# Squares between exps, squares in place, two tiles transposed by DMA, and masks by halves in a fused attention and MLP kernel

## The chip, the cores and the metric

One core of a Trainium2 chip. The metric is the device time of a whole execution in microseconds (us), lower is better. The kernel before takes 318.52 us (median of four runs, 317.75 to 319.37). Each ratio below is the mean time of one kernel's fast runs over that of the other's of the same rounds, on the same chip, so it is not quite the ratio of the medians that are quoted. "Same" means within 2%.

## The reference, cut to what matters

```python
# q, k, v: [8 batches, 8 heads, 576, 64]; s: [8, 8, 576]; w_in: [512, 2048]; w_out: [2048, 512]
scores = q @ k.T / 8                      # per batch and head
cum = cumsum(max(s, 0)); bias = -(cum[i] - cum[j])
scores = where(causal, -1e9, scores + min(bias, 0))
attn = softmax(scores)                    # + 1e-9 in the denominator
x = (attn @ v) as [4608 tokens, 512]
out = gelu(x @ w_in) @ w_out              # exact gelu
```

## The kernel before

The MLP runs in nine chunks of 512 tokens. Its first layer (`l1_item`) needs `xT`, the attention's output transposed; its second layer (`l2_item`) is cut into 16 pieces, and between these pieces stand the attention items of a later batch: in chunk c's second layer that is batch b = c+1. `sc` computes scores and two exps, `mk` masks them, `av` multiplies with v and normalises, `to_xT` transposes one tile of 128 tokens, on TensorE or, for most tiles, by DMA. A batch has 576 tokens and a chunk 512, so the first layer of chunk 1 needs tiles 0 to 3 of batch 1, and that of chunk 2 tiles 0 to 2 of batch 2.

ScalarE also squares q and k of batch 0 and all of v, only for their sums, which a check of the inputs' size uses at the end. The squares' output itself is thrown away:

```python
def square_v(b, st):
    n_st = 128 if st < ST - 1 else SL
    sq = work.tile([128, S * 2], bf16, tag="sq", bufs=1, name="sq")
    nc.scalar.activation(sq[:n_st, : H * D], raws[b, "v"]..., func=AF.Square,
                         accum_out=sumv[:n_st, b, st : st + 1])
# second layer of chunk 0 (b = 1), cut
side[6] = [(scale_v, b, 2), (av, b, 1, 0, True), (mk, b, 0, 1)]
side[7] = [(sc, b, 1, 1), (av, b, 1, 1, True), (to_xT, b, 0, True)]      # True: on TensorE
side[8] = [(scale_v, b, 3), (av, b, 0, 2), (to_xT, b, 1, True), (gelu_set,), (mk, b, 1, 1)]
# second layers of chunks 1 to 6 (b = 2 to 7), cut
sc_at = (2, 5, 7, 9) if b < 4 else (2, 5, 8, 11)
...
for st in range(ST):
    side[sc_at[3]].append((square_v, b, st))
side[sc_at[3]].append((gelu_set,))
```

The loads of v have two buffers. The load for the batch after next waits until the last reader of its buffer is done, and in these chunks that reader is the fifth square. All loads are issued in order on the GpSimd queue; stores and DMA transposes on the sync queue.

## Time and profile before

| | before |
|---|---|
| time, median of 4 runs | 318.52 us |
| span of the profiled run | 316.6 us |
| TensorE busy | 303.5 us |
| clock of TensorE granted in the profile | 1.00 (0.994 to 0.999 in later runs) |

TensorE is busy 96% of the span, so a change must be read by what TensorE waits for.

### The profile page before, as it was taken

Reading aid. Unit: us, or ns where it says so; the run is one execution under the profiler, and the core shown is the slowest. Engines: PE = TensorE matmul, PEld = TensorE weight load, DVE = VectorE, ACT = ScalarE, POOL = GpSimd, SP = SyncE. Lnnn points to the kernel's source line nnn. Section 1 sums busy time; section 2 is a strip of 40 time slices with the busy share of each in tenths; the row PEclk is TensorE's granted clock in tenths of the full one; section 3 lists DMA queues with packets and bytes.
Section 4 is the critical chain, followed back from the end, with each engine's and each line's share of the span. In section 5 each row is a group of like instructions: output and inputs, shape, how many; then the busy total and the mean of one; then the engine's idle time right before and its main releaser. Section 6 shows DMA issues by size and latency. Waiting matters only on the chain. (4 is left out here: it accounts for less than half of the span.)

```text
span 316.6 us, 6078 instructions
## 1 busy us (share of the span) xinstructions
PE 303.5 (96%) x2480; PEld 156.1 (49%) x2523; DVE 199.9 (63%) x400; ACT 192.9 (61%) x256; POOL 52.9 (17%) x72
## 2 busy tenths in 40 slices
PE   8999998999999999999999999999999999999993
PEld 3587754444554455445444444444444545444441
DVE  7876658699769766965697559945894632250020
ACT  2786976887765687564956676657756685105500
POOL 8543440125070006000240004000000000000000
PEclk9999999999999999999999999999999999999999
DMA  7999999669869215932399158412110321010012
GB/s 133 220 230 209 226 212 277 129 111 211 187 176 185 64 53 155 196 59 76 97 176 162 66 101 160 35 56 79 52 24 34 101 51 25 33 69 33 1 69 75
DMA packets 30980, 36.48 MB, mean 115 GB/s; under 512 B 15648, under 2 KB 20000, under 8 KB 30944
## 3 DMA queue, kind: packets, MB, share of 16 engines
q0 software_dynamic: 11552, 23.07, 38.5%
q1 hardware_dynamic: 19248, 12.80, 15.7%
q8 instruction: 22, 0.36, 0.5%
q14 instruction: 14, 0.11, 0.2%
q10 hardware_dynamic: 144, 0.13, 0.1%
HBM read 36.85 MB, written 9.44 MB: 146 GB/s over the span
## 5 line engine op out<-in xcount | busy, mean ns | idle before, releaser
L466 PE MATMUL h_ps<-xT,w_in_r 128*128 128x512 bf16 (+1 forms) x626 | 131.7, 357 | 2.8 <-ACT gT L471 2.0
L482 PE MATMUL o_ps<-w_out_r,gT 128*128 128x512 bf16 x549 | 132.3, 379 | 2.2 <-issue 1.3
L471 ACT ACTIVATE gT<-h_ps 128x1024 bf16<-128x1024 f32 (+1 forms) x80 | 74.6, 938 | 63.7 <-PE h_ps L466 62.9
L466 PEld LDWEIGHTS <-w_in_r 128*128 128x128 bf16 x640 | 60.0, 98 | 56.5 <-issue 2.9
L482 PEld LDWEIGHTS <-gT 128*128 128x128 bf16 x576 | 52.0, 98 | 56.5 <-issue 3.1
L358 ACT ACTIVATE P<-sc_ps 128x1024 bf16<-128x1024 f32 x56 | 54.3, 1021 | 30.7 <-PE sc_ps L343 30.7
L122 POOL DMA_DIRECT2D raw_v<-in_v_dram x40 | 34.0, 864 | 119.7 <-ACT sq L212 107.4
L492 DVE COPY o_sb<-o_ps 128x512 f32<-128x512 f32 x32 | 22.1, 691 | 48.5 <-PE o_ps L482 48.5
L443 DVE RECIPROCAL rc<-av 128x4 f32<-128x4 f32 (+1 forms) x80 | 14.0, 175 | 40.2 <-PE av L434 40.2
L187 DVE STREAM_TRANSPOSE qkT<-raw_qk 128x576 f32<-128x576 f32 x32 | 37.4, 1242 | 0.9 <-DMA raw_qk<-in_k_dram 0.6
L434 PEld LDWEIGHTS <-P 128*128 128x128 bf16 x576 | 27.2, 98 | 17.4 <-DVE x L444 1.6
L444 DVE TENSOR_TENSOR x<-av,rc 128x256 bf16<-128x256 f32 (+1 forms) x80 | 33.8, 423 | 3.0
L204 DVE TENSOR_REDUCE amx<-raw_qk 128x2 f32<-128x2304 bf16 x14 | 35.1, 2535 | 0.0
L434 PE MATMUL av<-vv,P 128*128 128x65 bf16 x576 | 30.4, 193 | 1.0 <-DVE x L444 0.7
L220 DVE TENSOR_TENSOR vv<-raw_v,wb 128x512 bf16<-128x512 f32 (+1 forms) x40 | 26.0, 689 | 3.2 <-DMA raw_v<-in_v_dram 3.2
L366 DVE TENSOR_TENSOR P<-P,tri_bf 128x1024 bf16<-128x1024 bf16 x32 | 21.9, 684 | 8.8 <-ACT P L358 8.8
L212 ACT ACTIVATE sq<-raw_v 128x512 bf16<-128x512 f32 (+1 forms) x40 | 25.1, 628 | 0.8
L343 PE MATMUL sc_ps<-qkT 32*128 32x256 bf16 (+2 forms) x560 | 18.2, 250 | 0.1
L343 PEld LDWEIGHTS <-qkT 32*128 32x128 bf16 x560 | 11.7, 92 | 12.7 <-issue 12.0
L418 PE MATMUL f_ps<-zero 128*128 128x512 bf16 x32 | 11.2, 468 | 1.3 <-DVE zero L150 1.2
L497 ACT ACT_TABLE_LOAD x8 | 10.3, 1283 | 0.9 <-PEq L819 0.7
L500 ACT ACT_TABLE_LOAD x8 | 10.3, 1283 | 0.1
(79 smaller groups left out, 90.2 us busy)
## 6 DMA issues: line engine op xcount, KB each, us to landing
out_dram<-o_sb SPq DMA_DIRECT2D x35, 256.0 KB, 2.2
raw_v<-in_v_dram POOLq DMA_DIRECT2D x32, 256.0 KB, 6.3
raw_qk<-in_q_dram POOLq DMA_DIRECT2D x7, 576.0 KB, 9.0
raw_qk<-in_k_dram POOLq DMA_DIRECT2D x7, 576.0 KB, 11.9
w_in_r<-in_moe_w_in_dram POOLq DMA_DIRECT2D x4, 512.0 KB, 12.0
w_out_r<-in_moe_w_out_dram POOLq DMA_DIRECT2D x4, 512.0 KB, 16.4
raw_v<-in_v_dram POOLq DMA_DIRECT2D x8, 128.0 KB, 8.0
raw_qk<-in_q_dram POOLq DMA_DIRECT2D x2, 288.0 KB, 5.6
```

The costliest lines, as they stand in the source:

```text
L122: eng.dma_start(out=t[:n_st, st, :, :], in_=bass.AP(tensor=v.tensor, offset=v.offset + b * H * S * D + st * 128 * D, ap=[[D, n_st], [S * D ...
L187: nc.vector.transpose(qkT[b % 2][:, i, g, :S, :].rearrange("p s e -> p (s e)").bitcast(fp32) .rearrange("p (l j) -> p j l", j=LT), raws[b, ...
L204: nc.vector.tensor_reduce(amx[:, b * HG + g], raws[b, "qk"][:, :, g, :], axis=AX, op=ALU.max, apply_absolute_value=True,)
L212: nc.scalar.activation(sq[:n_st, : H * D], raws[b, "v"][:n_st, st].rearrange("p h d -> p (h d)"), func=AF.Square, accum_out=sumv[:n_st, b, ...
L220: nc.vector.tensor_tensor(vv[b % 2][:n_st, st, :, 0:D], raws[b, "v"][:n_st, st, :, :], w.unsqueeze(2).to_broadcast([n_st, H, D]), op=MULT,)
L343: nc.tensor.matmul(s_ps[h // 2][:, h % 2, off : off + n], lhsT=qk[r, 1, g, jt * 128 : jt * 128 + 128, e], rhs=qk[r, 0, g, i0 : i0 + n, e], ...
L358: nc.scalar.activation(P[:, 2 * h2 : 2 * h2 + 2, o : o + 512], s_ps[h2], func=AF.Exp, scale=scale)
L434: nc.tensor.matmul(o_ps[:, h, :], lhsT=P[:, h, off : off + 128], rhs=vv[b % 2][:, jt, 4 * g + h, :], start=(i == 0), stop=(i == len(BLK[it ...
L444: nc.vector.tensor_tensor(x_of[b, it][:n, g * 256 : g * 256 + 256].rearrange("p (h d) -> p h d", d=D), o_ps[:n, :, 0:D], rc[:n].unsqueeze( ...
L466: nc.tensor.matmul(h_ps[:, i, :], lhsT=w_in_r[:, ko, ft * 128 : (ft + 1) * 128], rhs=xT[:, ko, c * NB + n0 : c * NB + n1], start=(ko == 0) ...
L471: nc.scalar.activation(gT_of[c][:, f2 * 2 : f2 * 2 + 2, n0:n1], h_ps, func=AF.Gelu)
L482: nc.tensor.matmul(y_of[c, sub], lhsT=gT[:, ft, sub * 128 : (sub + 1) * 128], rhs=w_out_r[:, ft, :], start=(ft == 0), stop=(ft == FT - 1),)
```

## The change

Its intent: to fill ScalarE's gaps between exps with the squares of v, so that the gelu after them starts earlier; to take eight transposes of batch 1 off TensorE; to shorten the start of batch 0. The squares of q and k in place free the room for two square buffers.

```diff
     def square_qk(g, i):
-        sq = work.tile([128, S * 2], bf16, tag="sq", bufs=1, name="sq")
+        r = raws[0, "qk"][:, i, g, :]
-            sq, raws[0, "qk"][:, i, g, :], func=AF.Square, scale=D ** -0.5,
+            r, r, func=AF.Square, scale=D ** -0.5,
     def square_v(b, st):
-        sq = work.tile([128, S * 2], bf16, tag="sq", bufs=1, name="sq")
+        sq = work.tile([128, H * D], bf16, tag="sq", bufs=2, name="sq")
     # start of batch 0 (cut): mask by halves, last scores behind the transposes, three fillers fewer
+    mk_item(0, 1, 0, 0, 2)
     av_item(0, 0, 1)
+    mk_item(0, 1, 0, 2, 4)
     sc_first(0, 1, (1,))
-    mk_item(0, 1, 0)
-    sc_first(1, 1, (0,))
+    filler(1)
     ...
     # second layer of chunk 0
-                side[6] = [(scale_v, b, 2), (av, b, 1, 0, True), (mk, b, 0, 1)]
-                side[7] = [(sc, b, 1, 1), (av, b, 1, 1, True), (to_xT, b, 0, True)]
-                side[8] = [(scale_v, b, 3), (av, b, 0, 2), (to_xT, b, 1, True), (gelu_set,), (mk, b, 1, 1)]
+                side[6] = [(av, b, 1, 0), (av, b, 1, 1), (scale_v, b, 2), (mk, b, 0, 1)]
+                side[7] = [(sc, b, 1, 1)]
+                side[8] = [(scale_v, b, 3), (av, b, 0, 2), (gelu_set,), (mk, b, 1, 1)]
     # second layers of chunks 1 to 6
-                for st in range(ST):
-                    side[sc_at[3]].append((square_v, b, st))
+                for st, at in zip(range(ST), (0, 1, 1, 2, 2)):
+                    side[sc_at[at]].append((square_v, b, st))
```

More of the change, by code (lines that the diff above doesn't have):

```diff
@@ L210, in square_v @@
         n_st = 128 if st < ST - 1 else SL
-        sq = work.tile([128, S * 2], bf16, tag="sq", bufs=1, name="sq")
+        sq = work.tile([128, H * D], bf16, tag="sq", bufs=2, name="sq")
         nc.scalar.activation(
-            sq[:n_st, : H * D], raws[b, "v"][:n_st, st].rearrange("p h d -> p (h d)"), func=AF.Square,
+            sq[:n_st], raws[b, "v"][:n_st, st].rearrange("p h d -> p (h d)"), func=AF.Square,
             accum_out=sumv[:n_st, b, st : st + 1],
@@ L360, in sc_item, with mk_item @@
             )
-    def mk_item(b, g, u):
+    def mk_item(b, g, u, h0=0, h1=4):
         P = P_of[b, g]
         o = UO[u]
-        d = P[:, :, o : o + 512].rearrange("p e (g c) -> p e g c", c=256)[:, :, :, 0:128]
+        d = P[:, h0:h1, o : o + 512].rearrange("p e (g c) -> p e g c", c=256)[:, :, :, 0:128]
         nc.vector.tensor_tensor(
-            d, d, tri_bf.unsqueeze(1).unsqueeze(1).to_broadcast([128, 4, 2, 128]), op=MULT
+            d, d, tri_bf.unsqueeze(1).unsqueeze(1).to_broadcast([128, h1 - h0, 2, 128]), op=MULT
         )
@@ L546 @@
     filler(1)
+    mk_item(0, 1, 0, 0, 2)
     av_item(0, 0, 1)
+    mk_item(0, 1, 0, 2, 4)
     sc_first(0, 1, (1,))
-    mk_item(0, 1, 0)
-    sc_first(1, 1, (0,))
+    filler(1)
     av_item(0, 1, 0)
     av_item(0, 1, 1)
+    sc_first(1, 1, (0,), 0)
+    to_xT(0, 0, True)
+    filler(1)
+    to_xT(0, 1, True)
     sc_first(1, 1, (1,), 0)
-    to_xT(0, 0, True)
-    filler(2)
-    to_xT(0, 1, True)
-    filler(2)
     mk_item(0, 0, 1)
```

## The prediction

> **What bounds the kernel now.** I read the busy shares first, then the list of waits, then the table of busy time by stretches, then the timeline of the stretches that the change touches, because an average cannot say what one small move is worth.
>
> ```profile
> PE 303.5 (96%) x2480; PEld 156.1 (49%) x2523; DVE 199.9 (63%) x400; ACT 192.9 (61%) x256; POOL 52.9 (17%) x72
> ...
> ACT gT L471 <- PE h_ps L466: 62.9, 61, 15.2
> ...
> PE h_ps L466 <- ACT gT L471: 2.0, 4, 0.5
> ...
> PE av L434 <- DVE x L444: 0.7, 1, 0.7
> ```
>
> TensorE is busy for 303.5 of 316.6 us, and the other engines spend most of their idle time waiting for it. So the change can win only by taking work off TensorE or by taking away one of its few waits. All its idle time is 13.1 us, of which some 6 us lie at the very start and in the tail, which the change doesn't touch (1.25 us in the first 10 us, 5.4 us in the last 27). The waits that the list names inside the kernel are four of 0.5 us for ScalarE's gelu and one of 0.7 us for VectorE. Even all of them together are far from 2% (6.4 us). The chain that ended last has six pieces within the last 0.7 us and says nothing of the middle. In the table by stretches, 36 to 56 us (second layer of chunk 0) has 19.05 us of TensorE in 20.0 and a DMA share of 1.10: there TensorE and the DMA engines are full at once.
>
> **What the Trainium skill says, and the trace.**
> 1. "TensorE: Matmul & The Clock Gate", table at its head: ScalarE and VectorE run their queue strictly in order. So a square put between two exps delays the later exp if it doesn't fit the gap. The trace agrees: the gelu's table load starts only 0.01 us after the last of five squares that stand before it.
> 2. "ScalarE: Activation LUTs", What ACT_TABLE_LOAD costs: about 1283 ns, and a drain of about 1380 ns. The load agrees (1283 ns). The drain does not show: the load at 156.25 ends at 157.53 and the gelu starts at 157.55. I use 1.28 us.
> 3. "VectorE: DVE Perf Modes", Side-by-side: some 150 cycles fixed per instruction, two results a cycle in the 2x mode. The masks fit: 684 ns for 1024 elements and 283 ns for 256, which is 0.52 ns per element and 0.15 us fixed. A mask of 512 should take 0.42 us, so two halves 0.84 us in place of 0.68.
> 4. "DMA: Bandwidth & Descriptors", Issuing engines are not separate DMA queues: all issuers' transfers share 16 engines and interleave. A DMA transpose (sync queue) lands 2.4 us after its issue where DMA is quiet (issues at 83.9, 116.7 us), but takes 7.7 us at 62.1, 11.1 at 94.7 and 10.8 at 127.6, amid loads at a share near or above 1. The one of 94.7 landed at 105.8; the loads' full stretch had ended at about 104.2. So under load it lands about when the backlog drains.
>
> **The change, part by part.**
>
> **(a) Squares of v, batches 4 to 7** (second layers of chunks 3 to 6). The timeline before:
>
> ```profile
> 150.67 1.94 ACT L358 ACTIVATE P<-sc_ps 128x1024 bf16<-128x1024 f32 x2 [1.70 <-PE sc_ps L343]
> ...
> 152.50 0.63 ACT L212 ACTIVATE sq<-raw_v 128x512 bf16<-128x512 f32 x1
> ...
> 155.51 0.63 ACT L212 ACTIVATE sq<-raw_v 64x512 bf16<-64x512 f32 x1
> ...
> 156.25 1.28 ACT L500 ACT_TABLE_LOAD   x1
> ...
> 157.55 1.94 ACT L471 ACTIVATE gT<-h_ps 128x1024 bf16<-128x1024 f32 x2
> ...
> 158.62 1.89 PE L466 MATMUL h_ps<-xT,w_in_r 128*128 128x512 bf16 x7 [0.50 <-ACT gT L471]
> ```
>
> Five squares at a pitch of 0.76 us (0.63 plus 0.19 for the accumulator's read, less overlap) push the first gelu to 157.55; by then two groups of first-layer results fill both score buffers, and TensorE waits 0.50 us. The timeline has the same at 158.6, 191.8, 224.9 and 258.1: 4 x 0.5 = 2.0 us. After the change the exps come at (2, 5, 8, 11), with gaps of 1.32, 1.70 and 1.70 us between them; one, two and two squares (0.76, 1.52, 1.52 us) fit. The table load moves to 152.5, the gelu is ready at 153.8, before its data. **-2.0 us.**
>
> **(b) Squares of v, batches 2 and 3** (second layers of chunks 1 and 2). Here the exps stand at (2, 5, 7, 9) and the gaps are shorter:
>
> ```profile
> 80.31 1.94 ACT L358 ACTIVATE P<-sc_ps 128x1024 bf16<-128x1024 f32 x2 [0.87 <-PE sc_ps L343]
> ...
> 82.28 0.66 PE L343 MATMUL sc_ps<-qkT 32*128 32x256 bf16 x24
> ...
> 82.96 1.94 ACT L358 ACTIVATE P<-sc_ps 128x1024 bf16<-128x1024 f32 x2 [0.71 <-PE sc_ps L343]
> ```
>
> Two squares (1.52 us) don't fit the gap of 0.87: the exps that started at 80.31 start at about 80.9 and end at 82.85. The next scores, at 82.28, need both score buffers that these exps free. So TensorE waits about 0.6 us where it waited for nothing. In chunk 2 the gap is 0.71 us: 0.8 us late, and scores at 115.16 against exps that ended at 115.12, so 0.7 to 0.75 us. The last exps become some 1.4 us late, but their masks are needed only at 86.9, just in time. The gelu had 1.2 us of idle time before it here, so nothing is won at the end. **+1.3 us.** Also, the last square frees the buffer for the loads of v some 4 us earlier (84.4 in place of 88.5). They then run beside the transposes of 83.9 and 85.2, which the next first layer needs at 89.7; by the store at 90.1, which took 3.4 us amid the same loads, I count on 0 to 0.5 us.
>
> **(c) First tiles of batch 1 by DMA** (second layer of chunk 0). It takes eight 128x128 transposes off TensorE: two groups of four at 0.24 us, 0.5 us. It takes two copies of 0.42 us off VectorE, and with them and the earlier second item the wait of 0.69 us at 48.75, where TensorE waited for an output buffer. Together 1.2 us off TensorE's path before chunk 1, whose first layer had begun at 56.4. But that layer reads columns 512 to 1023, which hold both tiles. The outputs should be ready at about 45.3 and 46.2, so the transposes issue at 45.3 and 46.5, in the middle of the loads: the share is 1.05 at 53, 0.96 at 54, 0.73 at 55 us. By the pattern in point 4 above they land at about 55.5 to 57.5, while TensorE would be ready at about 55. So a new wait of 0.5 to 2.5 us takes the place of what was removed. I take 1.3: **+0.1 us.**
>
> **(d) Start of batch 0.** From the first output item to the first layer at 18.93 there are seven filler matmuls before and four after, at 0.21 us: 0.65 us less. But the start of the layer hangs on VectorE: mask, reciprocal and scaling, transposes, copy (18.45 to 18.87). Halving the mask lets two heads begin early but costs 0.15 us, and the second half now follows the output of tile 1, so it ends at about 16.2 against 16.09. The last scores move behind the transposes, which takes 0.35 us out from in front of them; the first gelu comes about 0.8 us later, which four free buffers of 0.87 us each absorb. **-0.3 us**, uncertain by as much.
>
> **(e) Squares of q and k in place.** Same four instructions of 1.16 us at the same places, one buffer less; no wait in the list is for that buffer. The loads that wait for these squares (10.4 us on the queue) wait as before. **0.**
>
> Sum: -2.0 + 1.3 + 0.3 (loads beside transposes) + 0.1 - 0.3 = -0.6 us. 318.6 becomes **318.0 us**.
>
> **Rivals.**
> - *The DMA transposes come in time.* For it: the stores at 46.5 and 48.2, issued on the same queue under the same load, landed after 7.5 and 7.8 us, so 53 to 54.5 for the transposes. Against it: transposes move in small packets and were the slowest (11 us). Then (c) is worth -1.2 and the time is 316.8.
> - *The transposes are late twice*: at chunk 1 by 2.5 us, and at chunks 2 and 3 because the earlier loads catch them, 1 to 2 us each. For it: 11 us seen at 94.7. Against it: loads of v build their backlog only after some 2 us. Then the time is 320 to 322.
> - *The delayed exps cost nothing.* If the ends of exps and the start of scores have more slack than the modelled matmul times show, (b) is 0 and the time is about 316.7.
>
> **Range and chances.** Combined, the rivals give some 316 to 321; the runs before spread over 1.6 us. Eight in ten: **316.2 to 319.8**. Nothing reaches 6.4 us either way: faster 0.02, same 0.96, slower 0.02.
>
> **What would show it.** (a) is right if the list of waits has no more waits of the first layer for gelu at the start of chunks 4 to 7. (b) is right if the scores have new waits of 0.6 to 0.75 us for exps, twice. (c) is right if the first layer of chunk 1 waits for a DMA transpose of xT, with a landing of 9 to 11 us; it is wrong if it starts at 55 without a wait. (d) shows in the first layer's start against 18.93. The whole is wrong if TensorE's busy time moves by more than the 1.2 us of transposes and fillers, or if a wait of over 2 us appears elsewhere.

## More of the kernel before

From the 40-slice view of the page of before: a digit is the busy share of a slice of 7.9 us in tenths, and PEclk the granted clock in tenths.

```profile
PE   8999998999999999999999999999999999999993
...
PEclk9999999999999999999999999999999999999999
```

There is no slice in which TensorE is less than 80% busy before the tail, nor one with a lowered clock.

## The result, and the profile after

336.2 us (median of four runs, 334.22 to 337.84) against 318.52: ratio 1.0552, 95% interval 1.0488 to 1.0615. The change is 5.5% slower, and the prediction of 318.0 (316.2 to 319.8) was wrong.

The same views of the page after:

```profile
PE 308.1 (93%) x2470; PEld 156.8 (47%) x2512; DVE 199.4 (60%) x399; ACT 189.5 (57%) x256; POOL 52.9 (16%) x72
...
PE   8999996799979998699989998999999999999993
...
PEclk9999999799989999599999999999999999999999
```

TensorE's share fell to 93%, and in three places, at about 60, 98 and 136 us, the granted clock is lowered. TensorE's busy time rose by 4.6 us though it has fewer instructions: some matmuls ran longer. From the list of waits after (us in total, times, longest):

```profile
PE h_ps L467 <- issue: 8.1, 7, 4.0
PE h_ps L467 <- DMA xT<-x: 4.5, 1, 4.5
```

The four waits of 0.5 us for gelu are gone, as predicted. In their place the first layer waits for xT. The profile names the DMA only once; the other waits it puts down to "issue", which means that it found no releaser. The timeline fills that in. After, at the start of chunk 2:

```profile
88.57 4.21 POOL L122 DMA_DIRECT2D raw_v<-in_v_dram  x5 [8.80 <-ACT sq L213]
88.68 2.54 SPq L406 DMA_TRANSPOSE xT<-x  x2
...
96.23 3.03 PE L467 MATMUL h_ps<-xT,w_in_r 128*128 128x512 bf16 x8 [2.13 <-issue]
```

Before, at the same place in the program:

```profile
83.87 2.54 SPq L405 DMA_TRANSPOSE xT<-x  x2
...
88.82 4.20 POOL L122 DMA_DIRECT2D raw_v<-in_v_dram  x5 [13.62 <-ACT sq L212]
...
89.13 1.89 PE L466 MATMUL h_ps<-xT,w_in_r 128*128 128x512 bf16 x8
```

Before, the loads of v came 4.95 us after the first transpose, when both had landed (2.4 and 2.5 us after issue). After, they come 0.1 us before it. Its two transposes land 4.9 and 6.1 us after issue, the second at 96.1 us, and TensorE goes on at 96.23. In chunk 3 it is the same: the second transpose, issued at 127.3, lands 7.9 us later at 135.2, and TensorE goes on at 135.33 after 3.96 us. At the starts of chunks 4 and 5 waits of 0.70 and 0.69 us are left.

At chunk 1, whose tiles are now DMA transposes, the stretches of 2 us after (busy time of each engine with its instruction count, then granted clock, DMA share, GB/s):

```profile
56.00:58.00 2.00, 0.00 (x0) 0.00 (x0) 0.00 (x0) 0.01 (x1) 1.42 (x2) 1.00 1.28 130
58.00:60.00 2.00, 0.28 (x1) 0.14 (x2) 0.00 (x0) 0.00 (x0) 0.00 (x0) 0.82 1.14 242
60.00:62.00 2.00, 1.78 (x5) 0.76 (x5) 0.00 (x0) 0.60 (x1) 0.00 (x0) 0.50 1.10 293
62.00:64.00 2.00, 2.00 (x16) 0.90 (x14) 0.63 (x3) 0.91 (x1) 0.00 (x0) 0.83 1.12 212
```

TensorE stands still for 4.54 us until 59.72, and then the clock stays at half for about 3 us: five matmuls start in 60 to 62 us where eight take 1.89 us at full clock. (Three microseconds at half the clock do the work of 1.5 us; this first layer is 1.46 us longer than before.) VectorE does nothing from 56 to 60 us and ScalarE next to nothing; GpSimd works for 1.42 us.

**Where the 15.8 us of span went.** I cut both timelines at the first matmul of each layer of each chunk and subtracted.

| what | us |
|---|---|
| waits for xT at the starts of chunks 1 to 5: 4.54, 2.13, 3.96, 0.70, 0.69 | +12.0 |
| first layers of chunks 1, 2, 3 longer: 1.46, 1.66, 2.86 | +6.0 |
| second layers of chunks 1 to 4 longer beside these waits: 0.39, 0.61, 0.16, 0.17 | +1.3 |
| tail | +0.5 |
| first layers of chunks 4 to 7 shorter: 4 x 0.65 | -2.6 |
| second layer of chunk 0 without its wait | -1.0 |
| start and first layer of chunk 0 | -0.4 |
| sum | +15.8 |

### The profile page after: what moved, and what is told of

It reads as the page before. It is cut to its first block, busy times and chain, and to the rows that moved or that the text cites. A ratio compares the mean times of both kernels' runs of the same rounds, so it can differ in the third digit from the quotient of the medians.

```text
span 332.4 us, 6053 instructions
## 1 busy us (share of the span) xinstructions
PE 308.1 (93%) x2470; PEld 156.8 (47%) x2512; DVE 199.4 (60%) x399; ACT 189.5 (57%) x256; POOL 52.9 (16%) x72
## 5 line engine op out<-in xcount | busy, mean ns | idle before, releaser
L467 PE MATMUL h_ps<-xT,w_in_r 128*128 128x512 bf16 (+1 forms) x624 | 136.4, 367 | 13.6 <-issue 8.1
L493 DVE COPY o_sb<-o_ps 128x512 f32<-128x512 f32 x32 | 22.1, 691 | 47.6 <-PE o_ps L483 47.6
L435 PEld LDWEIGHTS <-P 128*128 128x128 bf16 x576 | 27.9, 99 | 17.8 <-issue 1.7
L367 DVE TENSOR_TENSOR P<-P,tri_bf 128x1024 bf16<-128x1024 bf16 (+1 forms) x33 | 22.1, 669 | 9.4 <-ACT P L359 9.4
L419 PE MATMUL f_ps<-zero 128*128 128x512 bf16 x29 | 9.5, 452 | 1.2 <-DVE zero L150 1.2
```

The lines of the kernel that those rows point to most:

```text
L435: nc.tensor.matmul(o_ps[:, h, :], lhsT=P[:, h, off : off + 128], rhs=vv[b % 2][:, jt, 4 * g + h, :], start=(i == 0), stop=(i == len(BLK[it ...
L467: nc.tensor.matmul(h_ps[:, i, :], lhsT=w_in_r[:, ko, ft * 128 : (ft + 1) * 128], rhs=xT[:, ko, c * NB + n0 : c * NB + n1], start=(ko == 0) ...
```

## The experiments

Theory after the result: DMA transposes that are in flight together with loads land late, the change makes that happen at three places where TensorE needs them at once, and each long wait also costs half the clock for some microseconds. Rivals: that the delayed exps are what costs; that one wait at chunk 1 shifts everything after it; that the longer first layers come from something other than the clock. All runs gave correct results.

### 1. The two tiles alone (t_tiles)

```diff
 # before, with the three lines of side[6], side[7] and side[8] of the change
```

> The kernel before with part (c) alone: the first two tiles of batch 1 go by DMA transpose. Theory: these transposes are issued at about 45.5 us into a full DMA queue and land some 13 us later, so the first layer of chunk 1 starts at about 60 us in place of 56.6 (a wait of about 4.5 us less 1.0 us of TensorE work removed), and the array's clock is then halved for about 3 us, which makes that first layer 1.5 us longer. Chunks 2 and 3 start without a wait for a transpose. Total about +4.8 us, 323 us. Rival (the three waits of the changed kernel are all a consequence of the first, because it shifts the loads against the transposes): then the waits at chunks 2 and 3 show here too and the time is near 334 us.

Measured: 325.71 us (323.51 to 326.14), ratio 1.0193 (1.0155 to 1.023). The wait is 6.1 us, the second layer of chunk 0 is 5.06 us longer, the first layer of chunk 1 2.31 us longer, and every later layer is within 0.15 us of before. So this part costs some 2% by itself, 6.2 us where I expected 4.8, and the waits at chunks 2 and 3 are not its consequence: that rival falls. Landing of its two transposes (us, least, median, most), from the view of that line:

```profile
DMA to landing us min/median/max: 14.3/14.8/15.4
```

### 2. The squares alone (t_squares)

```diff
-                for st in range(ST):
-                    side[sc_at[3]].append((square_v, b, st))
+                for st, at in zip(range(ST), (0, 1, 1, 2, 2)):
+                    side[sc_at[at]].append((square_v, b, st))
```

> The kernel before with the squares of v of batches 2 to 7 between the exps, and nothing else. Theory: the last square frees the buffer of v earlier, so the loads of v for the batch after next are issued at the same moment as the two DMA transposes of batches 2 and 3; the transposes land 5 to 8 us after issue in place of 2.5 us, the first layers of chunks 2 and 3 wait some 2 and 4 us, and the clock is halved after each wait (some 1.6 and 2.9 us). Against it stand 4 x 0.65 us won at the gelus of chunks 4 to 7. Total about +10.5 us, 329 us. Rival (delayed exps are what costs): waits of scores for exps, 0.6 and 0.7 us, no wait for a transpose, and a time near 317.5 us.

Measured: 325.2 us (323.87 to 327.59), ratio 1.0199 (1.0148 to 1.025). Where before the loads of v came 4.95 us after the first transpose of chunk 2, they now come with it, and the two transposes land after 5.0 and 6.4 us:

```profile
84.92 2.55 SPq L405 DMA_TRANSPOSE xT<-x  x2
84.96 4.22 POOL L122 DMA_DIRECT2D raw_v<-in_v_dram  x5 [9.10 <-ACT sq L212]
```

Its timeline of TensorE:

```profile
92.74 1.89 PE L466 MATMUL h_ps<-xT,w_in_r 128*128 128x512 bf16 x8 [2.40 <-issue]
119.36 0.64 PE L343 MATMUL sc_ps<-qkT 32*128 32x256 bf16 x22 [0.26 <-ACT P L358]
128.25 1.89 PE L466 MATMUL h_ps<-xT,w_in_r 128*128 128x512 bf16 x8 [1.89 <-issue]
196.17 3.28 PE L466 MATMUL h_ps<-xT,w_in_r 128*128 128x512 bf16 x8 [3.22 <-issue]
```

The waits at chunks 2 and 3 are there (2.40 and 1.89 us) and a third at chunk 5. Only after the one of 3.22 us was the clock lowered (eight matmuls in 3.28 us); after the other two the first layers had their usual 14.8 us. So the 4.5 us that I had taken from the changed kernel for the clock at chunks 2 and 3 did not come. Over the four runs this part costs some 6 us in place of 10.5; the profiled run is the slowest of them. The one wait of scores for exps that the list names is 0.26 us; beside the waits for xT the second layers of chunks 1 and 2 are 0.54 and 0.76 us longer than before.

The third wait does not fit the theory as it stands. At chunk 5 the loads of v were issued at 189.40, 1.84 us after the first transpose (187.56). That transpose took 4.4 us to land, the second one (188.8) 7.2 us, and yet DMA moved nothing from 187 to 188.6 us. The kernel before shows such a delay at the same place with no load in flight at all: its transposes of 182.0 and 183.3 us landed after 4.3 and 3.7 us, and its loads of v were issued only at 189.69. Its stretch after the first of them was issued (columns as above; the last two are DMA share and GB/s):

```profile
182.00:183.00 1.00, 1.00 (x13) 0.49 (x11) 0.57 (x2) 0.14 (x1) 0.00 (x0) 1.00 0.00 0
```

So a delay of some 2 us can arise without loads. Its cause stays open.

### 3. The fifth square left behind (t_fifth_late)

```diff
+                for st, at in zip(range(ST), (0, 1, 1, 2, 3)):     # t_squares has (0, 1, 1, 2, 2)
```

> As the run with the squares alone, but the fifth square of each batch stays behind the last exps, so that the buffer of v is freed, and the loads issued, about as late as in the kernel before; the exps are delayed as much as there in the third gap. Theory (load timing): no waits for transposes at chunks 2 and 3, all first layers but the first at full clock; the gelu waits of chunks 4 to 7 are gone (-2.6 us) and delayed exps cost 0.4 to 0.6 us twice; about 316.8 us. Rival (delayed exps): still some 5 us or more slower than before.

Measured: 317.3 us (316.92 to 317.64), ratio 0.9943 (0.992 to 0.9965). One square later turns 2% slower into 0.6% faster. Its timeline at chunk 2:

```profile
84.86 2.54 SPq L405 DMA_TRANSPOSE xT<-x  x2
...
86.78 4.22 POOL L122 DMA_DIRECT2D raw_v<-in_v_dram  x5 [10.99 <-ACT sq L212]
...
90.11 1.89 PE L466 MATMUL h_ps<-xT,w_in_r 128*128 128x512 bf16 x8
```

The loads now start 1.9 us after the first transpose in place of together with it. The transposes land after 2.4 and 2.5 us, though the second (issued at 86.2) was still in flight when the loads began, and no first layer waits for xT. The delayed exps stay but for one square fewer in the last gap, and cost 0.38 and 0.54 us in the second layers of chunks 1 and 2. The first layers of chunks 4 to 7 are 0.65 us shorter each, with a single square buffer. So the time of the loads was the cost, not the exps.

### 4. The start of batch 0, in place, two buffers (t_start)

```diff
 # the changed kernel with side[6] to side[8] and the squares' places as before
```

> The start of batch 0 alone (mask by halves, last scores behind the transposes, three fillers fewer), with the squares of q and k in place and the smaller square tile, all else as before. My step (d) gave -0.3 us; the changed kernel's trace has the first layer at 18.10 in place of 18.93 us, but 0.45 us of that is given back within chunk 0. So -0.4 us, 318.1 us, same within 2%. If squares in place cost anything, it shows here as a longer second layer of chunk 0 than 20.4 us.

Measured: 316.38 us (315.83 to 317.16), ratio 0.9916 (0.9891 to 0.9941). That is 2.3 us more than expected. The first layers of chunks 4 to 7 are 0.57 us shorter each, though the squares of v stand at their old place. This asked for the next run.

### 5. Two square buffers alone (t_buffers)

```diff
 # before, with the changed kernel's square_qk (in place) and square_v (two buffers), nothing else
```

> The kernel before with the squares of q and k in place and the square tile of v given two buffers; every instruction stays where it was. The run of the start alone won 0.57 us at each of the chunks 4 to 7 though the squares of v stood at their old place. Theory: the second buffer takes a bubble of 0.15 us out of each step from one square to the next (pitch 0.61 in place of 0.76 us), five squares end 0.7 us earlier, and the gelu after them no longer holds up TensorE: 4 x 0.57 us, total 316.3 us. Rival (the win came from the new start of batch 0, which shifts loads): then the pitch stays 0.76 us, the four waits of 0.5 us stay, and the time is 318.5 to 319 us.

Measured: 316.22 us (316.1 to 317.01), ratio 0.9918 (0.9891 to 0.9944). ScalarE's timeline at chunk 3, first before, then in this run:

```profile
152.50 0.63 ACT L212 ACTIVATE sq<-raw_v 128x512 bf16<-128x512 f32 x1
...
153.25 0.63 ACT L212 ACTIVATE sq<-raw_v 128x512 bf16<-128x512 f32 x1
```

```profile
152.48 0.63 ACT L212 ACTIVATE sq<-raw_v 128x512 bf16<-128x512 f32 x1
...
153.09 0.63 ACT L212 ACTIVATE sq<-raw_v 128x512 bf16<-128x512 f32 x1
...
155.66 1.28 ACT L500 ACT_TABLE_LOAD   x1
...
156.96 1.97 ACT L471 ACTIVATE gT<-h_ps 128x1024 bf16<-128x1024 f32 x2
```

The pitch of the squares is 0.61 us where it was 0.75 to 0.76, and the gelu starts at 156.96 where it started at 157.55. The first layers of chunks 4 to 7 are shorter by 0.57 or 0.58 us each, 2.3 us in all. So nearly all of what moving the squares wins (0.65 us each, as t_fifth_late shows) can be had from the second buffer alone, without a move. And since this run equals the one with the new start of batch 0, that start is worth nothing that can be measured here.

### 6. Fillers in the waits (t_warm)

```diff
+            if c in (1, 2, 3):
+                filler((20, 10, 18)[c - 1])
             for f2 in range(FT // 2):
                 l1_item(c, f2)
```

> The changed kernel with 20, 10 and 18 filler matmuls (0.21 us each) in front of the first layers of chunks 1, 2 and 3, in the waits for the transposes. Theory: the waits themselves stay, but the clock is not halved after them, so these first layers take 14.3, 14.8 and 14.8 us again in place of 15.8, 16.5 and 17.6: about 6 us less than the changed kernel, less some 0.5 us where a filler outlasts a wait: 330.5 us. Rival (the longer first layers come from something else, such as ScalarE's late start or loads in the memory): then these layers stay long and the time stays at 336 us.

Measured: 332.62 us (328.96 to 333.81, six runs), ratio to before 1.0446 (1.0413 to 1.0478), where the changed kernel has 1.0552. The three first layers take 14.29, 14.78 and 14.77 us again, as before the change, and the clock over the whole run is 0.994 to 1.0 in place of 0.973 to 0.979. So the longer first layers were the clock. The total fell by less than 6 us in most runs (the medians differ by 3.6 us); in the profiled run, the fastest, the second layer of chunk 2 with its filler took 1.1 us longer than in the changed kernel, because the second transpose landed after 9.0 us in place of 7.9. What the slower runs lost is not shown, as no trace of them was kept.

### 7. Loads of v held until the tile is ready (t_hold_v)

```diff
+    def hold():
+        nc.gpsimd.tensor_copy(hold_t, x_of[1, 1][:, 511:512])
+        load_v(2, nc.gpsimd)
 # on top of t_tiles: load_v(2) leaves its place; (hold,) stands behind the second av of side[6]
```

> Part (c) alone as in the run of the two tiles, but the loads of v of batch 2 are held until the second tile is ready (a one-column copy on the GpSimd queue, which reads that tile, is put before them), so the transposes do not queue behind them. Theory (the transposes starve behind a backlog of loads): they land 5 to 8 us after issue, by 54 us, the first layer of chunk 1 starts without a wait at about 55.5 us and at full clock: about 1 us faster than before, 317.5 us. Rival (DMA transposes are slow beside any load, or behind the q and k and weight loads that stay): still 9 us or more to land, a wait of 1.5 us or more, 320 us or more.

Measured: 323.94, 322.44, 317.74 and 324.21 us. Two of these count as slow by the rule of 1.5% above the fastest, so the ratio of the two fast ones (1.0032, 0.9958 to 1.0106) says little. In the profiled run, one of the slow ones, the transposes landed 10.7 and 12.3 us after issue and TensorE waited 4.2 us. The loads of v were now issued at 47.3 us, between the transposes of 46.2 and 47.6, so the two were still in flight together. This experiment decides nothing: its times spread over 6.5 us, the one trace is of a slow run, and in the run of 317.74 us the wait was probably short. The next asks more sharply.

### 8. All loads of batch 2 held until the transposes have landed (t_hold_landed)

```diff
+        nc.gpsimd.tensor_copy(hold_t, xT[:, 0, 703:705])     # last column of tile 0, first of tile 1
+        load_qks(2)
+        load_v(2, nc.gpsimd)
```

> Part (c) alone, with all loads of batch 2 (q, k and v) held until both DMA transposes have landed (a small copy on the GpSimd queue that reads the transposed columns stands before them). Holding v alone did not help: the transposes still took 11 to 12 us, and the DMA engines moved only 50 to 90 GB/s at 50 to 54 us. Theory (a transpose and loads in flight together slow each other): with nothing but the last weights beside them the transposes land within 5 us, the first layer of chunk 1 starts without a wait for xT at about 55.5 us and its clock is not halved; but the loads come some 14 us later, so VectorE's transposes of q and k of batch 2 wait for them and the total is 317 to 319 us. Rival (transposes at this point are slow by themselves, whatever is loaded): 9 us or more again, and a wait of over 2 us for xT.

Measured: 318.97 us (318.54 to 319.19), ratio 1.0003 (0.9971 to 1.0035). The same view as for t_tiles:

```profile
DMA to landing us min/median/max: 3.3/3.7/4.2
```

3.3 and 4.2 us in place of 14.3 and 15.4, and no wait for xT: the second layer of chunk 0 is 1.19 us shorter than before. At this place, then, the transposes are not slow by themselves: with the loads of batch 2 out of the way some 11 us of their delay are gone. But the wait comes back later: the loads now come about 14 us late, VectorE's work on batch 2 with them, and in the second layer of chunk 1 (1.52 us longer) TensorE waits for a mask:

```profile
79.09 0.30 PE L434 MATMUL av<-vv,P 128*128 128x65 bf16 x4 [1.61 <-DVE P L366]
```

### 9. DMA transposes that nobody needs (t_dummy)

```diff
+    def dummy(it):     # columns of batch 7, written again later
+        nc.sync.dma_start_transpose(out=xT[:, :, 7 * S + it * 128 : 7 * S + it * 128 + 128], in_=x_of[1, it])
 # before, with (dummy, 0) and (dummy, 1) behind the two av items of batch 1, both av in side[6]
```

> The kernel before, which still transposes the tiles of batch 1 on TensorE, plus two DMA transposes of the same tiles at the same moment as in the changed kernel, into columns of xT that batch 7 fills later, so that nobody waits for them. Theory (transposes and loads slow each other): the two land 12 to 14 us after issue, the loads of v of batch 2 and the stores that were issued at 46 to 53 us land later than in the kernel before (median store 7.5, loads 12.7 us there), the DMA engines move clearly under 250 GB/s at 50 to 55 us (over 300 before), and the time is as before within 1%, since no instruction needs the result. Rival (only the transposes suffer, being served last): loads and stores land as before.

Measured: 320.59 us (319.33 to 322.19), ratio 1.0075 (1.0031 to 1.0119). The two transposes took 12.7 us in the median. DMA issues at 45 to 57 us (times, size, median us to landing), first before, then with the two transposes added:

```profile
out_dram<-o_sb SPq DMA_DIRECT2D x3, 256.0 KB, 7.5
raw_v<-in_v_dram POOLq DMA_DIRECT2D x1, 256.0 KB, 12.7
```

```profile
out_dram<-o_sb SPq DMA_DIRECT2D x3, 256.0 KB, 11.7
raw_v<-in_v_dram POOLq DMA_DIRECT2D x1, 256.0 KB, 12.8
```

The stores, which share the sync queue with the transposes, land 4 us later. The load of v lands as before. At 52 to 54 us DMA moved 212 GB/s in place of 345. So theory and rival are each half right: beside the transposes the stores of their queue are late and the rate is lower, but the loads that were ahead came on time. The late store also cost time: ScalarE waited 2.57 us for a store's buffer before its copy, and TensorE then 1.45 us for the gelu. By what mechanism loads delay a transpose so much stays open. These runs show that its 12 to 15 us at this place go away with the loads; they do not show that loads are the only cause of a late transpose (see chunk 5 in run 2).

### 10. A version meant to be better (t_best)

```diff
 # t_start, and:
+                for st, at in zip(range(ST), (0, 1, 1, 2, 3) if b >= 4 else (3,) * 5):
```

> A version meant to be better: the start of batch 0, the squares in place and the two buffers as in the changed kernel; the tiles of batch 1 transposed on TensorE as before; the squares of batches 2 and 3 behind the last exps as before; those of batches 4 to 7 between the exps except the fifth, which stays behind them so that the loads start as late as before. Theory: against the run of the start alone (0.9916 of before) only 4 x 0.08 us more at the gelus, so 0.990 to 0.991 of before, 316 us. If moved squares were worth something beyond the second buffer, it would be below 315.5 us.

Measured: 316.46 us (315.05 to 317.12), ratio 0.9904 (0.9873 to 0.9935). It beats both kernels, but not the two buffers alone, by any margin these runs resolve. Two buffers are the simplest version with the whole gain.

## Why the prediction was wrong, point by point

- **What bounds the kernel** held: TensorE does, and every microsecond lost or won is one of its waits or its clock.
- **(a)** was right in mechanism and near in size: the four gelu waits went, -2.6 us in place of -2.0. The move alone, with one buffer, gives this in t_fifth_late. What it missed is that a second buffer without a move gives -2.3 us, without the cost of (b).
- **(b), the exps**: predicted +1.3 us, measured 0.39 and 0.61 us in the changed kernel, 0.38 and 0.54 with the fifth square late: a little too large. The waits of scores for exps that were to show it, 0.6 to 0.75 us twice, are not in the list of the changed kernel, so this cost is read from the length of the layers.
- **(b), "I count on 0 to 0.5 us"** for transposes beside the earlier loads is a step that failed. It saw the collision but sized it by a store that took 3.4 us under such loads. The transposes took 4.6 to 7.9 us there, the waits were 2.13 and 3.96 us, and 1.4 us more at chunks 4 and 5, which it had not considered.
- **(c), "they land at about 55.5 to 57.5"** is the other. The backlog was taken from the trace without these transposes, as if they added nothing. They landed at 59.3 and 59.6; the wait was 4.54 us in place of the 1.3 taken. The gain side was right: -1.2 us predicted, -1.19 measured in t_hold_landed, where nothing waits for xT, and -1.04 in the changed kernel beside the wait.
- **No step of the sum had the clock.** Waits were counted at their own length. The halved clock added 6.0 us to three first layers, and t_warm gave the layers back their old length. The prediction's own sign against it came true: TensorE's busy time moved by 4.6 us, more than the 1.2 us of transposes and fillers.
- **(d)** -0.3 us: -0.4 in the profile after, nothing in the timed pair t_start and t_buffers (316.38 and 316.22 us). Not resolved: in kernels whose start is unchanged, the first layer begins anywhere from 18.93 to 19.94 us.
- **(e), "0"**, with its reason "no wait in the list is for that buffer", was said of the squares of q and k; the second buffer for the squares of v has no step of its own. Yet the two together, unmoved, are worth -2.3 us (t_buffers). The bubble of 0.15 us between squares is no entry of the list of waits; it shows only in the pitch of two squares, which the prediction used as a constant.
- **The rivals**: the second one, late transposes twice, is what happened. It was given 320 to 322 us; its waits were undersized and it too lacked the clock.

## What to carry to other kernels

When an engine off the critical path is moved, look up which buffer its last instruction frees and which transfer starts then, and what is in flight at that moment; here one square moved by some microseconds decided between 2% slower and 0.6% faster. Put a transfer that is needed at once where nothing else is in flight, or leave it on the engine; size a collision by a transfer of the same kind under the same load, and allow for a lowered clock after a TensorE wait of 2 us or more (here it followed waits of 2.13 us and of 3.2 to 6.1 us, but not those of 1.89 and 2.40). And look at the pitch of repeated instructions, not only at waits, for a missing second buffer.

## What the Trainium skill lacked or had wrong

- "TensorE: Matmul & The Clock Gate", Why this matters for your kernels, advises no idle gaps above about 3 us to avoid the lower clock. Here a wait of 2.13 us (chunk 2 of the changed kernel) was followed by a clock of 0.50 from 97 to 100 us. Waits of 2.40 and 1.89 us in t_squares were not. So one gap well below 3 us was enough, and the length of a gap alone does not decide.
- "Advanced Engine Details and Errata", X-Bar Transpose (TRN2), says that transposing DMAs are as fast as regular ones. In quiet stretches one usually lands after 2.4 us, but it moves 128 KB, and a store of 256 KB takes 2.2 us; in the kernel before one took 4.3 us with nothing else in flight. Together with loads they took 12.7 to 15.4 us (changed kernel and t_tiles) from some 46 us of the span, where stores took 7.5, and 3.3 to 4.2 us at the same place with the loads held. That section gives no time for a transpose beside loads.
- "Perfetto Trace Analysis", Optimization Strategy, says that the same gap repeating can mean too few buffers. No page that I read gives the size of the gap where an output buffer is used again at once, and here it is no entry of the list of waits: 0.75 to 0.76 us from square to square with one buffer, 0.61 us with two.
